# Attention and two feed-forward stages in one kernel: weight sums of the seven-product scheme taken in batch 0, one of two split anew in each batch

## The chip, the cores and the metric

One Trainium2 chip, one core. The metric is the device time of one execution in microseconds, the median of several runs.

## The reference

For 4 batches of 576 tokens with 8 heads of 64, causal attention is mixed with a memory read-out, and the result x (2304 x 512) goes through two feed-forward stages, all in float32:

```python
x = (g * mem_out + (1 - g) * local)                 # attention, 8 heads of 64 -> 512
h = (x @ w1) * (x @ w2) @ w3 @ w_out                # 512 -> 1024 -> 1024 -> 512
out = (sigmoid(x2 @ w_gate) * (x2 @ w_val)) @ w_out2  # x2 = h; 512 -> 1536 -> 512
```

## The kernel before

Float32 products are made from three fp32r matmuls: each operand is split into a high part (a cast) and a low part (the value minus the cast, `split_rows`, line 469), and high x high, low x high and high x low are summed in PSUM.

The work is four batches, one after the other (`ffn(b)`, line 506). Each has four stages that TensorE does in order: ab (x with w1 and w2, 8 tiles of 128 columns), xw (with w3 times w_out, multiplied ahead in `prep`), gv (with w_gate and w_val, 12 tiles) and ot (with the last matrix). The attention of batch b+1 is cut into small steps, which `drive` (line 943) puts between the products of ab, xw and ot of batch b; gv takes none. Batch 0 also loads all weights in their raw form, converts them (`conv_step`, line 204: VectorE, ScalarE and GpSimd in turn, into one of three buffers `wraw`), splits them (`split_step`, line 309) into a ring of slots for TensorE and stores the split form in DRAM (tiles `k`), from where the later batches fetch it (`load_step`, line 289). `pump` (line 342) takes one step of each after every product or two.

A tile of ab or gv has two weight blocks, one for each factor, and two halves of the tokens. With eight products that is 48 matmuls. The seven-product scheme (`two_rows`, line 417) needs 42, with sums of x (`token_steps`, line 395: eleven steps of subtraction and split) and, for each of 20 weight tiles, sums of the weights: four instructions (lines 270 to 273 in `make_step`), of which `lower` gives three to VectorE and one to GpSimd here. A tile then reads four slots: the plain first block, two slots with sums, and a plain block of half size. Its products come in the order 1, 6, 5, 2, 7, 3, 4: the first slot serves products 1 and 2, the second 6 and 5, the third 7 and 3, the fourth 4.

Before, batch 0 uses eight products everywhere and stores the raw weights of the 20 tiles too (`kf`, line 241). In batch 1, `make_step` fetches them (`wagain`), makes the sums, splits them into `wmade` buffers (tag r64, three of them, which parts 4 to 6 of the tokens' sums use too) and stores them (`s`, line 281), a tile's two sum slots as two transfers of 512 KB. So gv of batch 1 has seven products and ab of batch 1 has eight; batches 2 and 3 have seven in both and fetch both sum slots ready (line 302). In batches 2 and 3 the three `wraw` buffers serve as more slots, eight in all; in batch 1 there are five (`RING`).

Tile pools set who waits: a new tile in a buffer waits for the last reader of the old one. Instructions are put in order by a scheduler on all engines but TensorE, whose order from batch 0 on is the written one. All transfers are issued from SP's queue, in order.

Of the kernel before, what the change touches and what calls it, by code (L numbers as in the profile page):

```python
# [35 lines left out]
SHARE_W = (0.2, 0.5, 0.5, 0.0)  # L36
SHARE_H = (0.0, 0.0, 0.3, 0.4)
# [3 lines left out]
SHARE_S = (0.0, 0.0, 0.5, 0.0)  # L41
# [12 lines left out]
def tile_attention_memory_ffn(  # L54
# [74 lines left out]
    kept = {}  # L129
    summed = {}  # L130
    plain = {"ab": [], "xw": [], "ot": []}
    seven = {"ab": [], "gv": []}

    def unit(src, stage=None, ring=True):
        u = len(units)
        if stage:
            ks = []
            for hf in range(2):
                n = 2 * u + hf
                nb = 2 if stage == "gv" and hf == 1 else 4  # L140
# [1 line left out]
                ks.append(stored[n])
            if stage in plain:
                plain[stage] += [(t, 4, None) for t in ks]
            if stage in seven:
                kept[u] = dr.tile([128, 8, 128], F32, tag=f"kf{u}", name=f"kf{u}")
                summed[u] = [
                    dr.tile([128, 2, 4, 128], F32, tag=f"s{u}_{m}", name=f"s{u}_{m}") for m in range(2)
                ]
                a22 = ks[1] if stage == "gv" else ks[1][:, :, 2:4]  # L150
                seven[stage] += [(ks[0], 4, None), (summed[u][0], 4, u), (summed[u][1], 4, u), (a22, 2, None)]
# [24 lines left out]
    makes = [x[2] for st in ("gv", "ab") for x in seven[st][1::4]]  # L176
    second = plain["ab"] + plain["xw"] + seven["gv"] + plain["ot"]
    NSECOND = len(second)
    again = second + (seven["ab"] + plain["xw"] + seven["gv"] + plain["ot"]) * (B - 2)
# [69 lines left out]
    made = set()

    def load_kept(k):
        if k < len(makes):
            t = fp.tile([128, 8, 128], F32, tag="wraw", name=f"wagain{k}", bufs=3)
            nc.sync.dma_start(out=t, in_=kept[makes[k]])
# [2 lines left out]
    def make_step():


        k = len(made)  # L260
        if k >= len(makes):
            return False
        if ws["mstep"] == 0:
            if k == 0:
                assert not raws
                for n in range(3):
                    load_kept(n)
            a11, a12, a21, a22 = (fresh[k][:, 2 * n : 2 * n + 2] for n in range(4))
            e1, e2 = lower(SHARE_S), lower(SHARE_S)
            e1.tensor_add(a22, a21, a22)  # L270
            e2.tensor_sub(a21, a11, a21)
            e1.tensor_sub(a11, a22, a11)
            e1.tensor_sub(a12, a12, a11)
            ws["mstep"] = 1
            return True
        m = ws["mstep"] - 1
        t = fp.tile([128, 2, 4, 128], F32R, tag="r64", name=f"wmade{k}_{m}", bufs=R64)
        src = fresh[k].rearrange("p (a b) c -> p a (b c)", b=2)
        src = src[:, 0::3] if m == 0 else src[:, 1:3]
        split_rows(t.rearrange("p x (a b) c -> p x a (b c)", b=2), src, SHARE_W)  # L280
        nc.sync.dma_start(out=summed[makes[k]][m], in_=t.bitcast(F32))
        ws["mstep"] = (ws["mstep"] + 1) % 3
        if m == 1:
            made.add(makes[k])
            del fresh[k]
            load_kept(k + 3)
        return True

    def load_step():
        m = ws["again"]  # L290
        if m >= len(again):
            return False
        src, nb, u = again[m]
        late = m - NSECOND
        tag, bufs = ("wslot", RING) if late < 0 or late % (RING + 3) < RING else ("wraw", 3)
        if sum(places[x] == tag for x in slots) >= bufs:
            return False
        while u is not None and u not in made:
            make_step()
# [206 lines left out]
    def ffn(b):  # L506
        fa, fw, fo = (*FR0, 1.0) if b == 0 else (FA[b > 1], 1.0, 1.0)
        x = Xops if b > 1 else Xt

        hs = []  # L510
        for f in range(F1):
# [123 lines left out]
    def attention(b, lag):  # L635
# [238 lines left out]
        def l_part(p):  # L874
# [205 lines left out]
```

## Time and profile before

| | |
|---|---|
| median of 3 runs | 1109.21 us (1105.85 to 1110.59) |
| profiled execution, its own time | 1108.51 us |
| its span | 1106.7 us |
| TensorE (matmul) busy | 1032.6 us, 93% |
| VectorE, ScalarE, GpSimd busy | 693.2, 541.0, 521.2 us |
| moved by transfers | 281.51 MB, mean 254 GB/s |

The span runs from the first to the last instruction; the execution's own time has the launch around it. The shares are means over stages with different limits, so the stretches are read apart. PE is TensorE's matmul, PEld its weight load, DVE VectorE, ACT ScalarE, POOL GpSimd, SP the queue that issues transfers. In a row of a timeline, the bracket tells how long the engine stood idle ahead and what ended that.

### The profile page before, as it was taken

The page shows a single profiled execution, that of the slowest core. Times are in us where ns is not written, and L with a number is a line of the kernel's source. Part 1 is how long each engine was busy: PE and PEld are TensorE (multiplying, and loading weights), DVE is VectorE, ACT ScalarE, POOL GpSimd, SP SyncE. Part 2 cuts the span into 40 slices and gives each one's busy share as a digit, 9 for nine tenths or more (in the row PEclk, how much of TensorE's full clock was granted, in tenths as well). Part 3 has the DMA queues.
Part 4 walks back from the last instruction along what each step waited for, and adds up shares of the span by engine and source line. Part 5 has one row for each costly group of instructions (what it writes and reads, how often), then busy time and mean ns, then how long its engine had stood idle before and what let it go on. Part 6 is the DMA issues. An engine that isn't in the chain of part 4 may idle for free.

```text
span 1106.7 us, 20533 instructions
## 1 busy us (share of the span) xinstructions
PE 1032.6 (93%) x7304; PEld 915.1 (83%) x7304; DVE 693.2 (63%) x1566; ACT 541.0 (49%) x1174; POOL 521.2 (47%) x452
## 2 busy tenths in 40 slices
PE   6989798999999799999769999999999999999998
PEld 3555586887989789898759989987999889999998
DVE  7896898867678846877845531786466524615630
ACT  6777565645565644655533342444544432224420
POOL 5887565525656644555733322554433422324320
PEclk9999889998999899999979999999999999999999
DMA  7565579956899569989978845875389537958981
GB/s 271 164 208 197 183 262 325 328 196 240 276 320 335 202 214 390 348 330 339 347 264 315 299 146 182 281 241 176 118 298 327 196 117 253 327 202 283 329 287 56
DMA packets 103934, 281.51 MB, mean 254 GB/s; under 512 B 12568, under 2 KB 35224, under 8 KB 103832
## 3 DMA queue, kind: packets, MB, share of 16 engines
q1 hardware_dynamic: 103832, 280.20, 73.8%
q8 instruction: 58, 0.95, 0.3%
q14 instruction: 44, 0.36, 0.1%
HBM read 211.48 MB, written 68.68 MB: 253 GB/s over the span
## 4 chain that ended last, share of the span: by engine, by line
PE 65%; DVE 14%; POOL 7%; DMA 5%; issue 5%; ACT 3%; SPq 0%; DVEq 0%; POOLq 0%; ACTq 0%
PE gvp L388 16%; PE ot L377 13%; PE abp L388 8%; PE ab L377 7%; PE xw L377 5%; PE s L738 4%; PE t L799 3%; PE o L867 3%; DVE wraw L235 2%; DVE wraw L234 2%; POOL wraw L239 2%; PE wps L377 2%; POOL x L472 2%; DMA wslot<-s 2%; DVE p L743 1%
## 5 line engine op out<-in xcount | busy, mean ns | idle before, releaser
L388 PE MATMUL gvp<-x,wslot 128*128 128x288 f32 x1512 | 208.1, 298 | 22.7 <-ACT x L470 14.9
L388 PEld LDWEIGHTS gvp<-x,wslot 128*128 128x128 f32 x1512 | 204.4, 190 | 26.1 <-ACT x L470 15.1
L377 PE MATMUL ot<-hg,wslot 128*128 128x288 f32 x1152 | 166.5, 301 | 4.3 <-DVE hg L472 4.3
L377 PEld LDWEIGHTS ot<-hg,wslot 128*128 128x128 f32 x1152 | 156.2, 190 | 10.6 <-issue 5.1
L769 POOL TENSOR_SCALAR p<-p,sm,omg 116x116 f32<-116x116 f32 (+4 forms) x100 | 93.7, 940 | 144.2 <-DVE sm L767 101.8
L239 POOL TENSOR_TENSOR wraw<-wraw,cr 128x512 int32<-128x512 int32 x76 | 110.8, 1469 | 75.8 <-DVE wraw L235 40.0
L108 ACT ACTIVATE p<-p,sm 116x116 f32<-116x116 f32 (+4 forms) x160 | 93.0, 582 | 71.6 <-DVE sm L743 71.4
L377 PE MATMUL ab<-x,wslot 128*128 128x288 f32 x768 | 120.1, 307 | 0.0
L377 PE MATMUL xw<-h,wslot 128*128 128x288 f32 x768 | 115.0, 303 | 1.7 <-DVE h L472 1.3
L377 PEld LDWEIGHTS ab<-x,wslot 128*128 128x128 f32 x768 | 106.4, 192 | 7.6 <-issue 4.9
L377 PEld LDWEIGHTS xw<-h,wslot 128*128 128x128 f32 x768 | 104.9, 191 | 7.0 <-issue 3.5
L743 DVE CUSTOM_DVE_ANT_0 p<-s,msk 116x116 f32<-116x116 f32 (+4 forms) x160 | 67.7, 452 | 52.1 <-PE s L738 51.8
L388 PE MATMUL abp<-x,wslot 128*128 128x288 f32 x672 | 96.1, 299 | 0.6 <-DVE u3ab L463 0.6
L388 PEld LDWEIGHTS abp<-x,wslot 128*128 128x128 f32 x672 | 90.3, 188 | 3.6 <-issue 1.3
L799 PE MATMUL t<-idf,p 116*116 116x116 f32 x480 | 70.8, 278 | 17.2 <-DVE p L769 10.3
L377 PE MATMUL gv<-x,wslot 128*128 128x288 f32 x576 | 79.3, 297 | 5.8 <-DVE hgraw L603 4.5
L377 PEld LDWEIGHTS gv<-x,wslot 128*128 128x128 f32 x576 | 76.7, 188 | 8.3 <-DVE hgraw L603 6.5
L799 PEld LDWEIGHTS t<-idf,p 116*116 116x116 f32 x480 | 55.3, 142 | 32.2 <-issue 17.7
L440 POOL TENSOR_TENSOR u4gv<-u2gv,s5gv 128x288 f32<-128x288 f32 x36 | 30.1, 836 | 73.5 <-ACT s5gv L438 73.5
L226 ACT ACTIVATE cr<-r 128x512 int32<-128x512 uint32 x76 | 51.2, 675 | 24.5 <-POOL wraw L239 24.0
L235 DVE SCALAR_TENSOR_TENSOR wraw<-cy,wraw 128x512 int32<-128x512 int32 x76 | 60.5, 820 | 0.2
L472 POOL TENSOR_TENSOR wslot<-wraw,wslot 128x512 fp32r<-128x512 f32 x36 | 51.7, 1437 | 17.8 <-ACT wslot L470 17.1
(124 smaller groups left out, 1741.2 us busy)
## 6 DMA issues: line engine op xcount, KB each, us to landing
wslot<-k SPq DMA_DIRECT2D x128, 512.0 KB, 5.0
wslot<-s SPq DMA_DIRECT2D x104, 512.0 KB, 4.7
k<-wslot SPq DMA_DIRECT2D x48, 512.0 KB, 4.7
s<-wmade SPq DMA_DIRECT2D x40, 512.0 KB, 5.9
wslot<-k SPq DMA_DIRECT2D x52, 256.0 KB, 4.3
r<-in_gv_dram SPq DMA_DIRECT2D x24, 512.0 KB, 6.2
kf<-wraw SPq DMA_DIRECT2D x20, 512.0 KB, 5.3
wagain<-kf SPq DMA_DIRECT2D x20, 512.0 KB, 6.8
```

Source lines behind the costliest of these rows:

```text
L108: ins = nc.scalar.activation(**kw)
L226: nc.scalar.activation(out=r, in_=w[:, :, 0].bitcast(U32), func=AF.Copy, scale=2.0**-29)
L235: nc.vector.scalar_tensor_tensor(z, y, -(2**31), z, ALU.bitwise_and, ALU.bitwise_or)
L239: nc.gpsimd.tensor_tensor(z, z, tmp["r"], ALU.add)
L377: nc.tensor.matmul(ps, w[:, wi, blk, :], x[:, xi, cols : cols + n], start=first and part == 0, stop=last and part == 2,)
L388: nc.tensor.matmul(ps, w[:, wi, blk + k, :], x[:, xi, k, :], start=k == 0 and part == 0, stop=k == 1 and part == 2,)
L472: eng.tensor_sub(dst[:, 1], src, dst[:, 0].bitcast(F32))
L738: nc.tensor.matmul(os_[hh], q_[r, 0, i * T : (i + 1) * T], k_[r, 1, c0:c1], start=x == 0, stop=x == len(terms) - 1,)
L743: nc.vector.tensor_tensor_reduce(out=ps_[hh][:, c0:c1], in0=os_[hh], in1=msk[:, SP - w + c0 : SP - w + c1], scale=-0.125, scalar=3.0e38 if ...
L769: lower(SHARE_N).tensor_scalar(ps_[hh][:, :w], ps_[hh][:, :w], sm[:, 6 + hh : 7 + hh], omg[:T, 2 * p + hh : 2 * p + hh + 1], ALU.mult, ALU ...
L799: nc.tensor.transpose(tp[:T, c : c + T], src[hh][:, j * T : (j + 1) * T], idf[:T, :T])
L867: nc.tensor.matmul(ot[r, XO + q0 : XO + S], v_[:, j, hh], pt[:, hh, j].rearrange("p a c -> p (a c)")[:, q0 - X : S - X] if j < 4 else pt[: ...
```

## The change

The sums are taken in batch 0, in place in `wraw`, right after the second half of a tile was split (`take_sums`), and stored in float32 instead of the raw weights. `make_step` and the `wmade` buffers are gone. In batch 1 the stored sums are fetched into `wraw` and both sum slots are split from there straight into the ring; the first of the two (`both`) is stored split, for batches 2 and 3. The second is split anew in batches 2 and 3 too, from half a fetch (256 KB). `wraw` serves for that, so the ring has five slots in all batches. Batch 1 has seven products in ab as well, and its x gets the sums that `two_rows` reads. The second slot of ab is stored at half size. The shares that `lower` deals by and one pace of `drive` are other numbers.

```diff
-SHARE_W = (0.2, 0.5, 0.5, 0.0)
-SHARE_H = (0.0, 0.0, 0.3, 0.4)
+SHARE_W = (0.2, 0.5, 0.5, 0.5)
+SHARE_H = (0.0, 0.0, 0.4, 0.4)
-SHARE_S = (0.0, 0.0, 0.5, 0.0)
+SHARE_S = (0.0, 0.5, 0.0, 0.0)
-FA = (1.0, 0.9)
+FA = (0.9, 0.9)
...
-                nb = 2 if stage == "gv" and hf == 1 else 4
+                nb = 2 if stage in ("ab", "gv") and hf == 1 else 4
...
+            if stage in ("ab", "gv"):
+                sums[u] = dr.tile([128, 8, 128], F32, tag=f"kf{u}", name=f"kf{u}")
+                both = dr.tile([128, 2, 4, 128], F32, tag=f"s{u}", name=f"s{u}")
+                ks[1:1] = [(both, u, 0), (None, u, 1)]
+            again[stage] += ks
...
+    again = [x for st in ("ab", "xw", "gv", "ot") for x in again[st]]
+    shared = list(sums)
+    again = again + [(x[0], 4) if len(x) == 3 and x[2] == 0 else x for x in again] * (B - 2)
...
-            if hf == 1 and u in kept:
-                nc.sync.dma_start(out=kept[u], in_=raws[u])
...
+    def take_sums(u):
+        a11, a12, a21, a22 = (raws[u][:, 2 * n : 2 * n + 2] for n in range(4))
+        e1, e2 = lower(SHARE_S), lower(SHARE_S)
+        e1.tensor_add(a22, a21, a22)
+        e2.tensor_sub(a21, a11, a21)
+        e1.tensor_sub(a11, a22, a11)
+        e1.tensor_sub(a12, a12, a11)
+        nc.sync.dma_start(out=sums[u], in_=raws[u])
+
+    def load_sums(k):
+        if k < len(shared) * (B - 1):
+            t = fp.tile([128, 8, 128], F32, tag="wraw", name=f"wsums{k}", bufs=3)
+            u = shared[k % len(shared)]
+            b0, b1 = (0, 8) if k < len(shared) else (2, 6)
+            nc.sync.dma_start(out=t[:, b0:b1], in_=sums[u][:, b0:b1])
             fresh[k] = t
...
     def load_step():
         m = ws["again"]
-        if m >= len(again):
+        if m >= len(again) or len(slots) >= RING:
             return False
...
+        w = fp.tile([128, 2, 4, 128], F32R, tag="wslot", name=f"wslot{n}", bufs=RING)
+        if len(again[m]) == 2:
+            src, nb = again[m]
+            w = w[:, :, :nb]
+            nc.sync.dma_start(out=w.bitcast(F32), in_=src)
+        else:
+            to, _, which = again[m]
+            k = ws["made"]
+            src = fresh[k].rearrange("p (a b) c -> p a (b c)", b=2)
+            src = src[:, 0::3] if which == 0 else src[:, 1:3]
+            split_rows(w.rearrange("p x (a b) c -> p x a (b c)", b=2), src, SHARE_W)
+            if to is not None:
+                nc.sync.dma_start(out=to, in_=w.bitcast(F32))
+            if which == 1:
+                del fresh[k]
+                ws["made"] += 1
+                load_sums(k + 3)
...
         if hf == 1:
+            if u in sums:
+                take_sums(u)
             del raws[u]
...
-        x = Xops if b > 1 else Xt
+        x = Xops if b > 0 else Xt
...
-            if b > 1:
+            if b > 0:
                 yield from two_rows(take(4), x, f"ab{b}_{f}", ht, hraw, False, 6.0 * fa)
...
-            while b == 1 and d == KC - 1 and make_step():
-                pass
...
-            if b == 1:
-                pending.append(lambda: tail(b, p, xp, SHARE_X))
-            elif p % 2 == 1:
+            if p % 2 == 1:
                 groups = token_steps(f"x{b}", *state["xf"], Xnext)
```

**Order, first place: VectorE in gv of batch 0**, one tile's time. `cy` and `wraw` belong to the conversion of a weight, `wslot` to its split, `hgraw` and `hg` to the products. Before:

```order
L603 TENSOR_TENSOR hgraw_3_3597<-gv_3_1_1_3660,gsb_3_1_3658 128x288
L472 TENSOR_TENSOR wslot_3698<-wraw_3515,wslot_3698 128x512
L234 TENSOR_SCALAR wraw_3695<-cy_3677 128x512
L234 TENSOR_SCALAR wraw_3695<-cy_3718 128x512
L472 TENSOR_TENSOR hg_3_3596<-hgraw_3_3597,hg_3_3596 128x576
L235 SCALAR_TENSOR_TENSOR wraw_3695<-cy_3677,wraw_3695 128x512
L235 SCALAR_TENSOR_TENSOR wraw_3695<-cy_3718,wraw_3695 128x512
L603 TENSOR_TENSOR hgraw_4_3687<-gv_4_0_1_3711,gsb_4_0_3709 128x288
L225 TENSOR_SCALAR cy_3808<-r_67_3681 128x512
L603 TENSOR_TENSOR hgraw_4_3687<-gv_4_1_1_3750,gsb_4_1_3748 128x288
L472 TENSOR_TENSOR wslot_3788<-wraw_3605,wslot_3788 128x512
```

Now:

```order
L227 TENSOR_SCALAR wraw_3917<-cy_3940 128x512
L581 TENSOR_TENSOR hgraw_7_4003<-gv_7_1_1_4065,gsb_7_1_4063 128x288
L228 SCALAR_TENSOR_TENSOR wraw_3917<-cy_3899,wraw_3917 128x512
L228 SCALAR_TENSOR_TENSOR wraw_3917<-cy_3940,wraw_3917 128x512
L244 TENSOR_TENSOR wraw_3823<-wraw_3823 128x256
L218 TENSOR_SCALAR cy_3993<-r_70_3850 128x512
L452 TENSOR_TENSOR hg_7_4002<-hgraw_7_4003,hg_7_4002 128x576
L581 TENSOR_TENSOR hgraw_8_4097<-gv_8_0_1_4121,gsb_8_0_4119 128x288
L452 TENSOR_TENSOR wslot_4108<-wraw_3917,wslot_4108 128x512
L246 TENSOR_TENSOR wraw_3823<-wraw_3823 128x256
L247 TENSOR_TENSOR wraw_3823<-wraw_3823 128x256
L581 TENSOR_TENSOR hgraw_8_4097<-gv_8_1_1_4159,gsb_8_1_4157 128x288
```

Three instructions on `wraw` of 128x256 have come in for each tile, on the buffer of the tile before the one that is converted.

**Second place: ScalarE at the start of gv in batch 1.** `x_1_0` to `x_1_6` are the seven parts of the tokens that the products need, `s1gv` and `s5gv` copies of products out of PSUM. Before:

```order
L470 CAST wmade_1_5991<-wagain_5828 128x512
L438 COPY s5gv_0_6646<-gvp_0_5_6639 128x288
L470 CAST wmade_0_6042<-wagain_5878 128x512
L470 CAST wmade_1_6067<-wagain_5878 128x512
L470 CAST wmade_0_6097<-wagain_5943 128x512
L470 CAST wmade_1_6127<-wagain_5943 128x512
L470 CAST x_1_4_6579<-x2f_1_6216 128x576
L470 CAST x_1_5_6612<-x2f_1_6216 128x576
L470 CAST x_1_6_6616<-x2f_1_6216 128x576
L108 ACT_TABLE_LOAD
```

Now:

```order
L450 CAST x_1_5_6495<-x2f_1_6001 128x576
L410 COPY s1gv_0_6511<-gvp_0_1_6504 128x288
L418 COPY s5gv_0_6529<-gvp_0_5_6522 128x288
L450 CAST wslot_6550<-wsums_5729 128x512
L450 CAST wslot_6563<-wsums_5729 128x512
L450 CAST x_1_6_6499<-x2f_1_6001 128x576
L108 ACT_TABLE_LOAD
```

The five casts into `wmade` ahead of x_1_4 to x_1_6 are gone; two casts into ring slots stand ahead of x_1_6.

**Third place: SP in gv of batch 3.** `s` is a sum slot that is fetched ready, `k` a plain slot, `kf` the stored sums. Before:

```order
L302 DMA wslot_12222<-s_0_156 128x1024
L302 DMA wslot_12211<-k_153 128x1024
L302 DMA wslot_12234<-s_1_157 128x1024
L302 DMA wslot_12250<-k_154 128x2x256
L302 DMA wslot_12291<-k_158 128x1024
L302 DMA wslot_12302<-s_0_161 128x1024
L302 DMA wslot_12314<-s_1_162 128x1024
L302 DMA wslot_12330<-k_159 128x2x256
L302 DMA wslot_12382<-s_0_166 128x1024
```

Now:

```order
L271 DMA wslot_9925<-k_142 128x2x256
L271 DMA wslot_9941<-k_145 128x1024
L271 DMA wslot_9982<-s_148 128x1024
L271 DMA wslot_10008<-k_146 128x2x256
L255 DMA wsums_9996<-kf_159 128x512
L271 DMA wslot_10024<-k_149 128x1024
L271 DMA wslot_10065<-s_152 128x1024
L255 DMA wsums_10079<-kf_163 128x512
L271 DMA wslot_10091<-k_150 128x2x256
```

Where two ready sum slots of 512 KB were fetched for a tile there is one now, and a fetch of 256 KB of unsplit sums into `wsums` for a tile three further on.

## Rows read from the trace of the kernel before

**Rows 1.** Table by stretch (us; busy time and count by engine, clock, DMA share, GB/s).

```profile
140.00:250.00 110.00, 103.68 (x714) 88.20 (x714) 86.29 (x188) 64.63 (x139) 54.95 (x45) 0.97 0.81 278
291.60:372.60 81.00, 75.77 (x552) 73.51 (x553) 63.93 (x102) 46.52 (x89) 49.98 (x34) 1.00 0.91 315
428.85:690.86 262.01, 240.06 (x1798) 218.62 (x1797) 163.15 (x376) 123.78 (x273) 117.07 (x103) 0.97 0.82 293
690.86:924.42 233.56, 230.18 (x1751) 210.02 (x1749) 131.97 (x346) 105.67 (x238) 97.06 (x89) 1.00 0.65 218
924.42:1103.20 178.78, 176.55 (x1322) 175.62 (x1320) 73.32 (x157) 51.94 (x108) 52.23 (x54) 1.00 0.75 256
```

**Rows 2.** Timeline of TensorE, gv of batch 1 (start, length, what, idle before).

```profile
545.10 1.23 PE L388 MATMUL gvp<-x,wslot 128*128 128x288 f32 x8
...
563.17 0.85 PE L388 MATMUL gvp<-x,wslot 128*128 128x288 f32 x2 [14.89 <-ACT x L470]
...
576.76 5.83 PE L388 MATMUL gvp<-x,wslot 128*128 128x288 f32 x42 [0.49 <-DMA wslot<-s]
...
595.29 11.43 PE L388 MATMUL gvp<-x,wslot 128*128 128x288 f32 x84 [0.99 <-DMA wslot<-s]
...
636.35 0.56 PE L377 MATMUL ot<-hg,wslot 128*128 128x288 f32 x3
```

**Rows 3.** Timeline of TensorE, gv of batch 2.

```profile
796.88 2.84 PE L388 MATMUL gvp<-x,wslot 128*128 128x288 f32 x20
...
804.18 62.40 PE L388 MATMUL gvp<-x,wslot 128*128 128x288 f32 x466 [0.92 <-POOL x L472]
866.42 0.56 PE L377 MATMUL ot<-hg,wslot 128*128 128x288 f32 x3
```

**Rows 4.** Timeline of ScalarE, start of gv in batch 1.

```profile
557.92 0.62 ACT L470 CAST wmade<-wagain 128x512 fp32r<-128x512 f32 x1 [1.95 <-DMA s<-wmade]
559.11 0.67 ACT L470 CAST x<-x2f 128x576 fp32r<-128x576 f32 x1 [0.57 <-DMA s<-wmade]
562.45 0.67 ACT L470 CAST x<-x2f 128x576 fp32r<-128x576 f32 x1 [2.66 <-DMA s<-wmade]
```

**Rows 5.** Costliest groups: GpSimd's part of a weight split (busy us, mean ns).

```profile
L472 POOL TENSOR_TENSOR wslot<-wraw,wslot 128x512 fp32r<-128x512 f32 x36 | 51.7, 1437 | 17.8 <-ACT wslot L470 17.1
```

**Rows 6.** Groups by line and shape: the sums, lines 270 to 273.

```profile
L271 POOL TENSOR_TENSOR wagain<-wagain 128x256 f32<-128x256 f32 x20 | 15.9, 794 | 28.4 <-DVE wagain L270 14.5 <-issue 10.6 <-DVE sm L767 1.5
...
L272 DVE TENSOR_TENSOR wagain<-wagain 128x256 f32<-128x256 f32 x20 | 14.3, 714 | 9.7 <-POOL wagain L271 9.7
...
L273 DVE TENSOR_TENSOR wagain<-wagain 128x256 f32<-128x256 f32 x20 | 13.0, 650 | 0.4
...
L270 DVE TENSOR_TENSOR wagain<-wagain 128x256 f32<-128x256 f32 x20 | 11.0, 551 | 8.9 <-DMA wagain<-kf 8.9
```

**Rows 7.** Timeline of TensorE, two tiles of gv in batch 0.

```profile
323.27 6.63 PE L377 MATMUL gv<-x,wslot 128*128 128x288 f32 x48 [0.49 <-DVE hgraw L603]
330.29 6.62 PE L377 MATMUL gv<-x,wslot 128*128 128x288 f32 x48 [0.40 <-DVE hgraw L603]
```

**Rows 8.** Timeline of VectorE, the same tiles of batch 0.

```profile
327.24 0.76 DVE L234 TENSOR_SCALAR wraw<-cy 128x512 int32<-128x512 int32 x2 [1.19 <-POOL wslot L472]
```

**Rows 9.** Instructions on tile wagain: ns shortest/median/longest, first and last start.

```profile
L272 DVE TENSOR_TENSOR wagain<-wagain x20: 408/426/1648, 405.0 to 553.8; 128x256 f32<-128x256 f32 x20
```

**Rows 10.** Chain of waits in gv of batch 1 (start, us, what).

```profile
572.30 4.32 DMA wslot<-s
...
578.62 4.11 DMA wslot<-s
...
590.33 4.82 DMA wslot<-s
```

**Rows 11.** Landing of tile wslot's transfers: 566 to 634 us, then 760 to 790.

```profile
DMA to landing us min/median/max: 3.1/4.3/5.6
...
DMA to landing us min/median/max: 3.0/3.2/3.6
```

More of the change, by code (lines that the diff above doesn't have):

```diff
@@ L128, in tile_attention_memory_ffn @@
     stored = {}
[L129 to L132, printed above, removed]
+    sums = {}
+    again = {"ab": [], "xw": [], "gv": [], "ot": []}
     def unit(src, stage=None, ring=True):
@@ L139, in unit @@
                 n = 2 * u + hf
-                nb = 2 if stage == "gv" and hf == 1 else 4
+                nb = 2 if stage in ("ab", "gv") and hf == 1 else 4
                 stored[n] = dr.tile([128, 2, nb, 128], F32, tag=f"k{n}", name=f"k{n}")
[L142 to L151, printed above, removed]
+                ks.append((stored[n], nb))
+            if stage in ("ab", "gv"):
[3 more added lines that the diff above has]
+            again[stage] += ks
         units.append((src, ring))
@@ L175, in tile_attention_memory_ffn @@
         unit(halves(o2[:, u]), "ot")
[L176 to L179, printed above, removed]
+    again = [x for st in ("ab", "xw", "gv", "ot") for x in again[st]]
+    shared = list(sums)
+    again = again + [(x[0], 4) if len(x) == 3 and x[2] == 0 else x for x in again] * (B - 2)
     NU = len(units)
@@ L186, in tile_attention_memory_ffn @@
     wot = {}
-    ws = {"conv": 0, "step": 0, "split": 0, "ring": 0, "freed": 0, "use": 0, "again": 0, "mstep": 0, "wo": 0, "pass": 0, "wready": False}
+    ws = {"conv": 0, "step": 0, "split": 0, "ring": 0, "freed": 0, "use": 0, "again": 0, "made": 0, "wo": 0, "pass": 0, "wready": False}
     tmp = {}
@@ L244, in conv_step @@
         return True
-    places = {}
     fresh = {}
[L249 to L254, printed above, removed]
-            fresh[k] = t
[L257 to L287, printed above, removed]
@@ L289, in load_step @@
     def load_step():
         m = ws["again"]
-        if m >= len(again):
+        if m >= len(again) or len(slots) >= RING:
             return False
[L293 to L299, printed above, removed]
-        n = ws["ring"]
-        w = fp.tile([128, 2, 4, 128], F32R, tag=tag, name=f"wslot{n}", bufs=bufs)[:, :, :nb]
@@ L302, in load_step @@
-        nc.sync.dma_start(out=w.bitcast(F32), in_=src)
+        if m == 0:
+            assert not raws
+            for k in range(3):
+                load_sums(k)
+        n = ws["ring"]
+        w = fp.tile([128, 2, 4, 128], F32R, tag="wslot", name=f"wslot{n}", bufs=RING)
[15 more added lines that the diff above has]
+                load_sums(k + 3)
@@ L303, in load_step @@
         slots[n] = w
-        places[n] = tag
         ws["ring"] += 1
@@ L334, in split_step @@
             slots[n] = w
-            places[n] = "wslot"
             ws["ring"] += 1
         if hf == 1:
+            if u in sums:
+                take_sums(u)
             del raws[u]
@@ L344, in pump @@
         split_step()
-        if phase["n"] == 2:
-            make_step()
     def need(store, s):
@@ L618, in ffn @@
                         pump()
-                        if pending:
+                        if pending and ws["conv"] >= NU:
                             pending.pop(0)()
@@ L1010, in tile_attention_memory_ffn @@
         phase["n"] = min(b + 1, 3)
-        ftot = 384 * FR0[0] + 144 * FR0[1] + 288 + 42.4 * (8 - NPREP) if b == 0 else (384, 336, 336)[b - 1] * FA[b > 1] + 432.0
+        ftot = 384 * FR0[0] + 144 * FR0[1] + 288 + 42.4 * (8 - NPREP) if b == 0 else 336 * FA[b > 1] + 432.0
         drive(ffn(b), chain(atts[b + 1], atts[b + 2]) if b + 1 < B else None, ftot, ATOT, FRAC)
```

## The prediction

> **What bounds the kernel now.** I first read the table of busy time by stretch [rows 1]. It cuts the part behind the start into two stretches of batch 0 and into batches 1, 2 and 3. In batches 2 and 3 TensorE is busy 230.2 of 233.6 us and 176.6 of 178.8 us: only fewer products could shorten them, and any new wait lengthens them. Batch 1 takes 262.0 us, 28.4 us more than batch 2, for the same work but for eight products in place of seven in its ab stage. Batch 0 is different: in its gv stage VectorE is busy 63.9 of 81.0 us, in its ab stage 86.3 of 110.0 us, the fullest of the engines beside TensorE.
>
> The timeline of TensorE says where batch 1 loses time. Its gv stage runs from 545.10 to 636.35, 91.25 us [rows 2]; that of batch 2 from 796.88 to 866.42, 69.54 us for the same 504 matmuls [rows 3]. One gap alone is 14.89 us, and ScalarE's cast of x ends it. ScalarE's timeline shows why [rows 4]: the casts of x wait for the stores of made sums (DMA s<-wmade), because both lie in the three buffers of tag r64. The rest of gv in batch 1 has gaps of 0.49 and 0.99 us that end with the fetch of a sum slot (wslot<-s) [rows 2]; batch 2, which had three more slots, has none in 62.40 us [rows 3].
>
> From 62.40 us for 466 matmuls [rows 3] I take 0.134 us for a matmul of 288 columns: seven products (42 matmuls) take 5.62 us, eight take 6.43 us.
>
> **Batch 1.** (a) The ab stage goes from 384 to 336 matmuls: 48 x 0.134 = **6.4 us less**, on TensorE's path. Its extra vector work is that of ab in batch 2, where TensorE hides it [rows 1]. (b) The sums are no longer made, stored and fetched in batch 1. The order of ScalarE shows x_1_4 and x_1_5 with no such cast ahead of them, and two casts ahead of x_1_6. With the makes gone, gv should come down to batch 2's 69.54 us: **21.7 us less**. (c) Not all of that stays. The cast of x_1_6 now stands behind a cast into a slot that TensorE frees only after its product 2: a cast (0.62 us [rows 4]), the cast of x and its subtraction come to some 2 us, with two products (1.6 us) and an old gap of 0.9 us [rows 3] against them; I take 1.3 us. And both sum slots of all 20 weight tiles are now split in front of their use: two casts of 0.62 us, one subtraction on VectorE and one on GpSimd (1437 ns, the same shape in batch 0 [rows 5]) in the 5.62 us of a tile. ScalarE and GpSimd have this time in batch 2's row (busy 106 and 97 of 234 us [rows 1]). What it costs is a product's evacuation that stands behind it; between 0 and one cast (0.62 us) for each tile I take 0.125 us, 2.5 us in all, near the lower end since three accumulators rotate and a product takes 0.8 us. **3.8 us more**. Batch 1 together: 24.3 us less.
>
> **Batch 0.** Sums for 20 tiles, 12 of gv and 8 of ab, move here. The same four instructions stood in batch 1 and have rows [rows 6]: on VectorE 551, 714 and 650 ns, 1.92 us a tile; on GpSimd 794 ns. In gv a tile now takes 7.02 us (from 323.27 to 330.29) where TensorE needs 6.43 [rows 7]. VectorE and GpSimd wait for each other in it: VectorE stands 1.19 us until GpSimd has ended a weight's subtraction, and only then rewrites a buffer [rows 8], to which GpSimd then adds. The change reorders this loop: a tile's buffer is now free only when its sums are stored, and the three sums of one tile stand on VectorE between the rewriting of two others. With 12 x 1.92 = 23 us added to 63.9 busy of 81.0, VectorE has at least 5.9 us too little in gv if every duration stays; the 8 tiles in ab (15.4 us) fit into its 23.7 idle us but stand in order in front of the products' evacuations. From below the cost is 0: with each sum at its shortest, near 0.41 us [rows 9], 12 x 1.23 = 15 us fit into the 17 idle ones. From above it is all 20 x 1.92 = 38 us. I take 8 us for gv (0.67 a tile, so a period near 7.7) and 4 us for ab, a quarter of its added work: **12 us more**, nearer the lower end because VectorE idles 1.5 us in each tile's period now. The GpSimd sum fits: GpSimd is busy 50 of 81 us. Token sums of batch 1's x (eleven steps in place of four splits) run in the last 22 us of batch 0's ot stage, where batch 2's are hidden already: 0. Stores of sums replace stores of raw weights one for one, and ab's second slot is stored at half size: 0 or a little gain.
>
> **Batches 2 and 3.** Now five slots serve where eight did. What is late then is the first sum slot. It goes into the buffer that product 2 frees, and product 6 of the next tile wants it. Batch 1 before had five slots, and its chain shows the pace [rows 10]: the fetch at 572.30 takes 4.32 us and work goes on at 576.76; the next is issued at 578.62, 1.86 us later. A tile needs 5.62 us, so a fetch of up to 3.76 us is hidden, and each us beyond is paid. In that stretch landings are 3.1/4.3/5.6 us (shortest, median, longest), with two fetches issued together; alone, in batch 2's xw stage, 3.0/3.2/3.6 [rows 11]. Now one 512 KB fetch stands there by itself, since the second sum slot is split from a buffer that was loaded three tiles ahead. I take 3.9 us, a little above the middle of the two medians: 0.14 us a tile. Tiles without attention between: 8 of ab in batch 3 and 24 of gv: 32 x 0.14 = **4.5 us more**. Bounds: 0 (3.2 us) and 32 x 1.06 = 34 us (4.82, the longest in the chain [rows 10]). The 40 new splits (half of them GpSimd's) lie beside products with 5.6 us for each. [...]
>
> **The sum.** Against the profiled execution's 1108.5 us (span 1106.7; the median of three is 1109.2): -6.4 - 21.7 + 3.8 + 12 + 4.5 = -7.8 us, so **1101 us**. 0.5% (5.5 us) is about what a measurement of this kernel can tell from no change.
>
> **The rivals.**
> 1. *Batch 0 gives everything back (slower).* Place: VectorE in ab and gv of batch 0. A sum there takes 0.41 us or up to 1.65 us [rows 9], the long ones under a GpSimd instruction; GpSimd is busy 62% of gv. If the sums are paid in full, +38 instead of +12: 1127 us. It decides from 20 us on, where the gain is gone. For it: 23 us of work against 17 idle; against it: VectorE's present waits are for GpSimd, and part of the sums falls into them. The Trainium skill (SBUF — State Buffer, Who interferes with whom) speaks for it: a VectorE instruction with two inputs in SBUF is blocked, not slowed, while GpSimd reads there. The trace agrees with 1.65 against 0.41 us. Chance 0.18.
> 2. *The ring of five is too short.* Fetches of 4.6 us, as paired ones had, cost 0.84 us in each of 32 tiles, 27 us instead of 4.5: 1123 us. For it: the gaps in batch 1; against it: less traffic at that moment. Chance 0.12.
> 3. *Batch 0 hides its sums.* VectorE's idle time takes them (+3), batches 2 and 3 lose 1 us: 1088 us. Chance 0.20.
> 4. *The change does not do what it says in batch 1*: splits in front of use hold x at the start of gv as the makes did, and 14 us of the gain stay away: 1115 us. The new order of ScalarE speaks against it. Chance 0.07.
> The forecast itself, 1094 to 1109, has 0.43.
>
> **How the numbers follow.** Faster by over 0.5% (below 1103.7): 0.30 of the forecast's 0.43 and all of rival 3, 0.50. Within: 0.13 of the forecast and 0.09 from the edges of rivals 1, 2 and 4, 0.22. Slower: the rest of rivals 1, 2 and 4, 0.28. For 8 in 10 the range leaves out the far halves of rivals 1 and 2 and the edge of 3: 1086 to 1124.
>
> **What would show it.** Right: batch 1 near 238 us with seven products in ab and no gap above 3 us at the start of gv; batch 0's gv at 7.5 to 8 us a tile; gaps of some 0.1 to 0.3 us that end with the fetch of a sum slot in gv of batches 2 and 3. Wrong: a period of 8.5 us or more in batch 0 with VectorE above 95% (rival 1), gaps of 0.8 us in every tile of batches 2 and 3 (rival 2), or the ab stage of batch 0 as long as before with gv at 7.0 us a tile (rival 3).

## The result and the profile after

The change makes the kernel slower by 1.1%: 1121.02 us (1118.84 to 1123.63, four runs) against 1108.97 (1105.85 to 1110.59, four), ratio 1.0113 [1.008, 1.0146]. Forecast: 1101. The profiled execution took 1122.1 us, its span 1120.3, 13.6 us longer than before.

Lengths of stages, here and in the experiments below, come from one profiled execution of each kernel. Where the code of a batch is the same they still differ: batches 2 and 3 took 433.1 us in the change, 430.8 in e3 and 433.2 in e6; batch 1 took 262.0 us before and 259.4 in e4. Differences of 2 to 3 us in a batch therefore say nothing by themselves.

Stage lengths from TensorE's timeline, from a stage's first product to the next stage's (before → after, us):

| | ab | xw | gv | ot | batch | forecast |
|---|---|---|---|---|---|---|
| batch 0 | 117.0 → 116.2 | 42.1 → 41.0 | 85.0 → 97.0 | 56.2 → 58.1 | +12.1 | +12 |
| batch 1 | 82.3 → 67.8 | 33.9 → 41.6 | 91.2 → 76.2 | 54.5 → 57.2 | −19.2 | −24.3 |
| batch 2 | 64.5 → 66.5 | 41.5 → 41.6 | 69.5 → 76.6 | 58.0 → 57.0 | +8.2 | } +4.5 |
| batch 3 | 44.8 → 50.1 | 26.1 → 26.8 | 69.5 → 76.1 | 38.3 → 38.3 | +12.5 | |

In batch 1, ab and xw have to be read together: attention steps moved from ab into xw (61 of their matmuls stand in xw before, 121 after).

The table of busy time by stretch, after (columns as in [rows 1]; first gv of batch 0, then batches 1, 2, 3):

```profile
291.60:372.60 81.00, 70.31 (x485) 67.50 (x484) 79.66 (x113) 38.65 (x74) 48.34 (x38) 0.96 0.77 265
441.04:683.84 242.80, 234.53 (x1751) 210.79 (x1749) 154.97 (x369) 124.79 (x279) 127.93 (x108) 1.00 0.65 220
683.84:925.63 241.79, 233.59 (x1750) 210.54 (x1749) 139.64 (x357) 116.30 (x258) 108.56 (x98) 1.00 0.59 188
925.63:1116.90 191.27, 181.79 (x1322) 177.53 (x1320) 79.84 (x167) 62.55 (x127) 64.36 (x63) 0.99 0.67 216
```

Against [rows 1], VectorE in gv of batch 0 went from 63.9 to 79.7 of 81.0 us: it is full, and TensorE does 485 matmuls where it did 552. TensorE stood idle 3.4 of 233.6 us in batch 2 and now 8.2 of 241.8, in batch 3 2.2 and now 9.5. That is 12.1 us of the 20.7 that these batches lost. The rest counts as busy time of the same matmuls: behind a gap the profile gives 42 of them 5.83 us, where a row without gaps gives them 5.62, and a part of gv in batch 3 ran at the lower clock (0.98 in that stage).

**Batch 0.** TensorE's timeline, gv of batch 0, after; these two tiles take 8.51 us each, from 312.01 to 320.52 and to 329.03, where one took 7.02 [rows 7]:

```profile
312.01 6.63 PE L357 MATMUL gv<-x,wslot 128*128 128x288 f32 x48 [1.34 <-DVE hgraw L581]
320.52 8.13 PE L357 MATMUL gv<-x,wslot 128*128 128x288 f32 x48 [1.88 <-DVE hgraw L581]
329.03 6.62 PE L357 MATMUL gv<-x,wslot 128*128 128x288 f32 x48 [0.37 <-DVE hgraw L581]
```

The middle tile spends 8.13 us on its 48 matmuls because TensorE ran part of it at the lower of its two clock levels, 1.2 GHz (granted clock 0.50 from 322.0 to 325.4), behind the gap of 1.88 us. That is not what lengthens the stage: in e5 the clock stays at 1.00 from 291.6 to 372.6, and gv of batch 0 takes 97.0 us too.

Groups by line and shape, after: the three of the four sums that VectorE does (count | busy us, mean ns | idle before).

```profile
L247 DVE TENSOR_TENSOR wraw<-wraw 128x256 f32<-128x256 f32 x20 | 14.2, 710 | 0.2
L246 DVE TENSOR_TENSOR wraw<-wraw 128x256 f32<-128x256 f32 x20 | 12.6, 629 | 2.7 <-POOL wraw L245 2.5
L244 DVE TENSOR_TENSOR wraw<-wraw 128x256 f32<-128x256 f32 x20 | 10.1, 507 | 2.6 <-POOL wslot L452 2.6
```

They take 1.85 us a tile on VectorE, as a mean of all 20 tiles; from [rows 6] 1.92 was expected. The size was right. Over the twelve tiles gv grew by 12.0 us, 1.0 us a tile: a little over half of these 1.85.

**Batch 1.** TensorE's timeline, start of gv, after (up to 565 us, where the last row is cut off):

```profile
550.41 2.94 PE L368 MATMUL gvp<-x,wslot 128*128 128x288 f32 x20
554.08 3.04 PE L368 MATMUL gvp<-x,wslot 128*128 128x288 f32 x18 [0.72 <-DVE x L452]
558.70 6.53 PE L368 MATMUL gvp<-x,wslot 128*128 128x288 f32 x47 [1.59 <-DVE x L452]
```

The gap of 14.89 us [rows 2] is gone; two gaps of 0.72 and 1.59 stand there. A slow stretch in and behind the old gap went with it: before, the granted clock was 0.50 (1.2 GHz) from 552.2 to 569.2, and the 21 matmuls from 563.17 on took 5.39 us. Later in that stage two rows of VectorE's timeline show a cost the forecast had at 0.125 us a tile:

```profile
606.66 1.87 DVE L452 TENSOR_TENSOR hg<-hgraw,hg 128x576 fp32r<-128x576 f32 x1
608.46 0.45 DVE L436 TENSOR_TENSOR u4gv<-gvp,u4gv 128x288 f32<-128x288 f32 x1
```

and one of GpSimd's, over the same time:

```profile
606.63 1.28 POOL L452 TENSOR_TENSOR wslot<-wsums,wslot 128x512 fp32r<-128x512 f32 x1
```

Here a new split's subtraction on GpSimd lies over VectorE's subtraction for hg, which takes 1.87 us; where GpSimd idles beside it 0.75 (gv of batch 2, VectorE's timeline):

```profile
833.78 0.75 DVE L452 TENSOR_TENSOR hg<-hgraw,hg 128x576 fp32r<-128x576 f32 x1
```

The product's evacuation u4 stands behind it, and TensorE's timeline in gv of batch 1 names u4:

```profile
608.96 5.89 PE L368 MATMUL gvp<-x,wslot 128*128 128x288 f32 x42 [0.37 <-DVE u4gv L436]
```

**Batches 2 and 3.** TensorE's timeline, gv of batch 2, after. In place of 62.40 us in one piece [rows 3] nearly every tile of 42 matmuls (5.83 us) has a gap:

```profile
820.04 5.83 PE L368 MATMUL gvp<-x,wslot 128*128 128x288 f32 x42 [0.37 <-DVE u3gv L443]
826.17 5.83 PE L368 MATMUL gvp<-x,wslot 128*128 128x288 f32 x42 [0.31 <-DMA wslot<-s]
832.25 5.83 PE L368 MATMUL gvp<-x,wslot 128*128 128x288 f32 x42 [0.26 <-DMA wslot<-s]
838.57 5.83 PE L368 MATMUL gvp<-x,wslot 128*128 128x288 f32 x42 [0.49 <-DVE hgraw L444]
```

The chain of waits there (start, us, what) alternates between two causes:

```profile
826.17 1.84 PE gvp L368 x12
828.03 4.09 DMA wslot<-s
...
832.25 2.65 PE gvp L368 x18
834.92 0.63 ACT wslot L450
835.55 0.07 issue
835.62 0.61 POOL wslot L452
836.23 0.64 issue
836.87 0.81 POOL s5gv L437
837.69 0.02 issue
837.71 0.45 DVE u3gv L443
838.16 0.38 DVE hgraw L444
```

First cause: 12 matmuls (products 6 and 5), then the fetch of the next first sum slot, then, 6.08 us after 826.17, product 6 of the next tile. Second: 18 matmuls (up to product 2), then the split of the second slot; s5 waits behind its subtraction on GpSimd, and u3 and hgraw, which free an accumulator, behind s5. The landings of wslot in this stretch (805 to 865 us), after:

```profile
DMA to landing us min/median/max: 3.4/4.3/5.7
```

The fetch of the sum slot is not alone in flight. SP's timeline has three other transfers within 4 us behind it, and the stage moves 245 GB/s:

```profile
828.03 0.32 SPq L271 DMA_DIRECT2D wslot<-s  x1
830.24 0.32 SPq L255 DMA_DIRECT2D wsums<-kf  x1
830.62 1.17 SPq L271 DMA_DIRECT2D wslot<-k  x2
```

TensorE's waits in batches 2 and 3, after (us in total, times, longest):

```profile
PE gvp L368 <- DMA wslot<-s: 2.9, 8, 0.6
...
PE gvp L368 <- DVE hgraw L444: 1.8, 4, 0.5
PE abp L368 <- DVE hraw L444: 1.8, 4, 0.5
...
PE abp L368 <- DMA wslot<-s: 1.0, 2, 0.6
```

With three single waits on L443 and L445 (0.4, 0.8 and 0.6 us), fetches of sum slots end ten gaps (3.9 us) and evacuations eleven (5.4 us). At the start of the two gv stages the waits for parts of x come to 5.5 us, where they were 3.6.

### The profile page after: what moved, and what is told of

It is laid out like the page before. It is cut to its first block, busy times and chain, and to the rows that moved or that the text cites. A ratio compares the mean times of both kernels' runs of the same rounds, so it can differ in the third digit from the quotient of the medians.

```text
span 1120.3 us, 20565 instructions
## 1 busy us (share of the span) xinstructions
PE 1045.5 (93%) x7256; PEld 915.7 (82%) x7256; DVE 747.8 (67%) x1629; ACT 562.2 (50%) x1217; POOL 578.1 (52%) x492
## 4 chain that ended last, share of the span: by engine, by line
PE 57%; DVE 21%; DMA 7%; issue 6%; ACT 4%; POOL 4%; SPq 0%; DVEq 0%; POOLq 0%; ACTq 0%
PE ot L357 13%; PE gvp L368 12%; PE xw L357 8%; PE abp L368 5%; PE ab L357 4%; PE s L716 4%; DMA wslot<-s 4%; PE t L777 3%; DVE wraw L228 3%; PE o L845 3%; DVE wraw L227 2%; PE wps L357 2%; DVE wslot L452 2%; DVE p L721 2%; DMA wslot<-k 2%
## 5 line engine op out<-in xcount | busy, mean ns | idle before, releaser
L368 PE MATMUL gvp<-x,wslot 128*128 128x288 f32 x1512 | 212.3, 299 | 16.9 <-DVE x L452 4.9
L357 PE MATMUL ot<-hg,wslot 128*128 128x288 f32 x1152 | 169.2, 302 | 6.0 <-DVE hg L452 3.8
L368 PE MATMUL abp<-x,wslot 128*128 128x288 f32 x1008 | 150.0, 300 | 5.2 <-DVE hraw L444 1.8
L368 PEld LDWEIGHTS abp<-x,wslot 128*128 128x128 f32 x1008 | 136.1, 188 | 13.6 <-DVE u3ab L443 3.3
L357 PE MATMUL xw<-h,wslot 128*128 128x288 f32 x768 | 116.2, 303 | 2.1 <-DMA wslot<-k 1.1
L357 PE MATMUL gv<-x,wslot 128*128 128x288 f32 x576 | 83.0, 304 | 11.8 <-DVE hgraw L581 11.3
L357 PEld LDWEIGHTS gv<-x,wslot 128*128 128x128 f32 x576 | 79.9, 195 | 14.8 <-DVE hgraw L581 14.2
L450 ACT CAST wslot<-wsums 128x512 fp32r<-128x512 f32 x80 | 48.9, 621 | 31.6 <-PE gvp L368 13.5
L228 DVE SCALAR_TENSOR_TENSOR wraw<-cy,wraw 128x512 int32<-128x512 int32 x76 | 63.8, 861 | 0.3
L357 PE MATMUL ab<-x,wslot 128*128 128x288 f32 x384 | 60.2, 309 | 1.3 <-DVE hraw L517 1.3
L452 POOL TENSOR_TENSOR wslot<-wsums,wslot 128x512 fp32r<-128x512 f32 x40 | 54.0, 1349 | 12.2 <-ACT wslot L450 11.9
```

The source lines that it names most:

```text
L228: nc.vector.scalar_tensor_tensor(z, y, -(2**31), z, ALU.bitwise_and, ALU.bitwise_or)
L357: nc.tensor.matmul(ps, w[:, wi, blk, :], x[:, xi, cols : cols + n], start=first and part == 0, stop=last and part == 2,)
L368: nc.tensor.matmul(ps, w[:, wi, blk + k, :], x[:, xi, k, :], start=k == 0 and part == 0, stop=k == 1 and part == 2,)
L450: nc.scalar.copy(dst[:, 0], src)
L452: eng.tensor_sub(dst[:, 1], src, dst[:, 0].bitcast(F32))
```

## The experiments

**e1, both slots fetched ready, five slots kept.** Batch 1 stores the second sum slot split as well; batches 2 and 3 split nothing.

```diff
-                both = dr.tile([128, 2, 4, 128], ...)
-                ks[1:1] = [(both, u, 0), (None, u, 1)]
+                both = [dr.tile([128, 2, 4, 128], ...) for m in range(2)]
+                ks[1:1] = [(both[0], u, 0), (both[1], u, 1)]
...
-    again = again + [(x[0], 4) if len(x) == 3 and x[2] == 0 else x for x in again] * (B - 2)
+    again = again + [(x[0], 4) if len(x) == 3 else x for x in again] * (B - 2)
...
-        if k < len(shared) * (B - 1):
+        if k < len(shared):
```

> The changed kernel, but batch 1 stores both sum slots split, and batches 2 and 3 fetch both ready: no split is left in batches 2 and 3, the ring keeps its five slots. The changed kernel lost 20.7 us in batches 2 and 3 (gv 76.6 and 76.1 us where it was 69.5 and 69.5, ab of batch 3 50.1 where it was 44.8). Theory F (the fetch of the first sum slot comes too late with five slots): gv stays at 75 to 78 us in both, the total at 1119 to 1125 us. Theory S (the new splits hold up the evacuation of products): gv goes back to 70 us, the total to 1100 to 1104 us.

Measured: 1131.57 us, ratio 1.0188 [1.0138, 1.0237]. Batches 2 and 3 took 426.0 us, against 433.1 in the change and 412.3 before: without the 40 splits they are 7.1 us shorter. Their gv took 72.9 and 74.3 us, between the two theories. But gv of batch 1 grew from 76.2 to 83.0 with the second store. The profiled execution took 1124.52 us, 7 us less than the median; where the other executions lost that time no trace shows.

**e2, e1 with eight slots in batches 2 and 3**, as before the change.

```diff
+        late = m - NSECOND
+        tag, bufs = ("wslot", RING) if late < 0 or late % (RING + 3) < RING else ("wraw", 3)
...
```

> As the run with both sum slots ready, and in batches 2 and 3 the three raw buffers serve as slots again, eight in all. Both theories: gv at 69.5 to 70.5 us in batches 2 and 3, the total at 1098 to 1103 us, under the kernel before, as batch 0 costs 12 us and batch 1 gives 19. If it stays above 1108 us, neither the ring nor the splits are the cause, and the change has hurt batches 2 and 3 in another way (the pace of the attention steps).

Measured: 1122.43 us, 1.0116 [1.0085, 1.0147]. Batches 2 and 3 took 414.1 us, gv 70.0 and 69.6: three slots more are worth 11.9 us, with both sum slots of a tile fetched, and 1.8 of the 20.7 are left. The total missed its forecast, since gv of batch 1 rose to 89.7 (83.0 in e1, whose code for batch 1 is the same; the difference is not explained). The chain of waits in gv of batch 1, e2, shows plain slots late:

```profile
565.58 6.60 DMA wslot<-k
580.24 7.24 DMA wslot<-k
596.22 7.81 DMA wslot<-k
```

Waits of SP's queue in gv of batch 1 (us in total, times, longest), the change:

```profile
SPq L280 <- DVE wslot L452: 36.3, 10, 5.2
```

and e2:

```profile
SPq L287 <- DVE wslot L460: 44.0, 11, 7.1
```

A store of a split slot waits at SP for the subtraction, and the fetches stand behind it in order. Either this queue or the second slot's bytes could make the fetches late; e7 asks which.

**e3, the sums' arithmetic left out**, everything else kept.

```diff
-        e1.tensor_add(a22, a21, a22)
-        e2.tensor_sub(a21, a11, a21)
-        e1.tensor_sub(a11, a22, a11)
-        e1.tensor_sub(a12, a12, a11)
```

> The changed kernel without the four instructions that take the sums in batch 0; the raw weights are stored in their place and split as if they were sums, so the products of batches 1 to 3 are others. Theory V (VectorE's time for the sums makes batch 0 longer): gv of batch 0 goes from 97 back to 85 to 87 us, the total to 1109 to 1112 us. Theory W (the raw buffer that is held until the store behind the split has landed makes it longer): gv of batch 0 stays at 93 to 97 us, the total at 1117 to 1121 us.

Measured: 1107.31 us, 0.998 [0.9962, 0.9998]. In gv of batch 0 (table by stretch, e3):

```profile
291.60:372.60 81.00, 75.68 (x551) 73.20 (x551) 62.28 (x100) 46.35 (x89) 49.76 (x35) 1.00 0.91 313
```

VectorE is back at 62.3 us, TensorE at 551 matmuls, the stage at 85.3. It is the sums' arithmetic that costs batch 0 its 12 us, and not the stores by themselves. The edit takes out GpSimd's sum too, and the stores' wait for the sums. So it does not tell VectorE's time from the longer time for which a tile's buffer is held.

**e4, the kernel before with five slots everywhere.**

```diff
-        tag, bufs = ("wslot", RING) if late < 0 or late % (RING + 3) < RING else ("wraw", 3)
+        tag, bufs = "wslot", RING
```

> The kernel before with five slots in batches 2 and 3 too, both sum slots fetched ready as it does: one edit. Theory F: gv of batches 2 and 3 at 75 to 78 us in place of 69.5, ab of batch 3 at 48 to 51 in place of 44.8, the total at 1125 to 1132 us. Theory S: no more than 1 to 3 us longer than the kernel before, 1109 to 1112 us.

Measured: 1123.02 us, 1.0108 [1.0066, 1.0151]. Batches 2 and 3 took 428.9 us, 16.5 more than before, with nothing else changed. That is over twice the 7.1 us that batches 0 and 1 together gain by the change, though here two sum slots are fetched for a tile, and in the change one.

**e5, the roles of the sum slots exchanged**: the first is split anew, the second stored.

```diff
-                ks[1:1] = [(both, u, 0), (None, u, 1)]
+                ks[1:1] = [(None, u, 0), (both, u, 1)]
...
```

> The changed kernel with the two sum slots exchanged in batches 2 and 3: the first one (products 6 and 5) is split anew from the raw buffer that was loaded three tiles ahead, the second one (products 7 and 3) is fetched ready. Ring of five, one split and one fetch of 512 KB a tile as before. Theory F (the fetch into the slot that frees last is late): that slot no longer waits for a fetch, so gv of batches 2 and 3 comes to 71 to 74 us in place of 76.6 and 76.1, ab of batch 3 to 46 to 48 in place of 50.1, the total to 1111 to 1116 us. Theory S (a split ahead of the evacuations is what costs): nothing is gained, 76 to 77 us, as in batch 1 where both are split (76.2), the total at 1119 to 1124 us.

Measured: 1122.97 us, 1.012 [1.009, 1.015]. Batches 2 and 3 gained 8.8 us (gv 74.2 and 72.7), batch 1 lost 10 (gv 86.5). In gv of batch 2 it is the plain first slot that is late now (chain of waits, e5):

```profile
816.15 5.76 DMA wslot<-k
827.92 5.78 DMA wslot<-k
```

So with five slots, in both roles, some fetch is short of lead; which one sets the price. Batch 1 lost its 10 us with one store a tile, as in the change, and at 233 GB/s in gv, where the change moves 276. Waits of SP's queue in that stage, e5:

```profile
SPq L273 <- DMA s<-wslot: 43.9, 10, 5.7
```

Fetches wait there for the store of a split slot to land. More bytes are not needed to make this stage long.

**e6, ScalarE takes all of the conversion's `cy` steps in batch 0.**

```diff
-SHARE_Y = (1.0, 0.4, 0.0, 0.0)
+SHARE_Y = (1.0, 1.0, 0.0, 0.0)
```

> The changed kernel with the first step of the conversion (cy) always on ScalarE in batch 0, where VectorE had six in ten of them. VectorE is busy 98% of gv in batch 0 with the sums, ScalarE 49%. Theory V: it takes 1.2 us a tile off VectorE, so gv of batch 0 goes from 97 to 88 to 92 us, the total to 1112 to 1117 us. Theory W (the held buffer and its store set the pace): gv stays at 95 us or more, the total at 1118 to 1122 us.

Measured: 1113.54 us, 1.0039 [1.0019, 1.0058], the total expected from relieving VectorE. The place was not: gv came down by 1.7 us only (97.0 to 95.3, and not at all in e8 and e10), VectorE still at 76.5 of 81.0:

```profile
291.60:372.60 81.00, 69.73 (x490) 66.72 (x490) 76.53 (x108) 46.68 (x89) 52.44 (x39) 0.98 0.84 280
```

Ten `cy` of 1.22 us are gone from VectorE in this stretch, but its subtraction for hg went from 1.02 to 1.30 us in the mean and the sum of L246 from 0.62 to 1.08. So VectorE's load alone does not set the length of gv. The rest came in ab, xw and ot of batch 0 (3.8, 2.9 and 4.5 us), less 4 us of a later start.

**e7, e2 with the stores issued later**, four calls of `pump` after the split.

```diff
-            if to is not None:
-                nc.sync.dma_start(out=to, in_=w.bitcast(F32))
+            if to is not None:
+                owing.append([4, to, w])
...
```

> The run with both sum slots ready and eight slots, with one edit: the stores of the split slots in batch 1 are issued four products later. In that run gv of batch 1 took 89.7 us in place of 76.2, with gaps that end with fetches of plain slots; SP stood 44 us in that stage waiting for a subtraction in front of a store, the fetches behind it. Theory Q (the queue: a store that waits for its split holds up the fetches behind it): gv of batch 1 at 74 to 78 us, the total at 1098 to 1104 us by the profiled execution. Theory B (the bytes: a store more in each tile is more than the transfers can carry): gv of batch 1 stays at 84 to 90 us, the total at 1108 to 1114.

Measured: 1118.64 us, 1.0105 [1.0071, 1.014]; gv of batch 1 91.1. SP waited as long as in e2 for subtractions:

```profile
SPq L338 <- DVE wslot L466: 45.0, 11, 6.6
```

The edit did not take away the wait that it was to test. Queue or bytes stays open for e2; e5 shows that this stage can get as long without more bytes.

**e8, e7 with e6.**

> The late stores and cy on ScalarE together. If theories V and Q both hold: batch 0 is 5 to 9 us shorter than in the changed kernel and gv of batch 1 no longer than there, the total at 1092 to 1098 us, faster than the kernel before by 1 to 1.5%. If only V holds 1103 to 1108, if neither 1112 or more.

Measured: 1111.07 us, 1.0002 [0.9981, 1.0024]. e6's edit gives the same on top of e7 (−7.6 us), and gv of batch 1 at 90.8 still eats the ring's gain.

**e9, product 2 right behind product 1** in `two_rows`, for all tiles of a stage but its first (whose x is not all ready then), with the plain slot released there and the first sum slot after product 5.

```diff
         p1 = product(1, 0, 0, 0)
...
+        p2 = product(2, 0, 2, 5)
+        release(s)
...
         p6 = product(6, 1, 0, 2)
...
         p5 = product(5, 1, 2, 1)
+        release(s + 1)
...
-        p2 = product(2, 0, 2, 5)
-        release(s)
-        release(s + 1)
```

> The changed kernel with product 2 done second in place of fourth, in every tile but the first of a stage: 1, 2, 6, 5, 7, 3, 4. The first slot is then free two products (1.6 us) sooner, and the slot that goes into its buffer has 5.6 us less its weight load in place of 3.8. Nothing else is moved. Theory F (the first sum slot's fetch has too little time with five slots): no gap in batches 2 and 3 ends with such a fetch, gv there at 70 to 73 us in place of 76.6 and 76.1, ab of batch 3 at 45 to 47 in place of 50.1, the total at 1105 to 1111 us. Theory S (the splits hold up evacuations): gv of batches 2 and 3 at 75 us or more, the total at 1118 to 1123 us.

Measured: 1112.78 us, 1.0029 [1.0015, 1.0042]; batches 2 and 3 425.5 us, 7.6 less than in the change. The gv stages took 75.6 and 72.1 us, ab of batch 3 48.1, so the expected 70 to 73 and 45 to 47 came only in part. ScalarE's timeline in gv of batch 2, e9, has the copies behind products 1 and 5:

```profile
825.14 0.40 ACT L410 COPY s1gv<-gvp 128x288 f32<-128x288 f32 x1 [0.65 <-PE gvp L368]
...
827.54 0.40 ACT L433 COPY s5gv<-gvp 128x288 f32<-128x288 f32 x1
```

and SP's has the fetch between them:

```profile
825.88 0.32 SPq L271 DMA_DIRECT2D wslot<-s  x1
```

In the change that fetch went out at 828.03, behind product 5. Now product 2 frees a slot before product 6 starts, the fetch has the whole tile of 5.6 us, and TensorE has rows of a hundred matmuls again:

```profile
798.46 20.90 PE L368 MATMUL gvp<-x,wslot 128*128 128x288 f32 x142 [0.58 <-DVE x L463]
...
820.02 15.47 PE L368 MATMUL gvp<-x,wslot 128*128 128x288 f32 x114 [0.66 <-DVE c11gv L416]
```

No gap in these gv stages ends with hgraw any more either, though a tile's split still starts behind its fourth product; why is not shown.

**e10, e9 with e6.**

> Product 2 second and, in batch 0, cy on ScalarE, which alone made the changed kernel 7.5 us faster. If both are independent: 1098 to 1104 us, faster than the kernel before by 0.5 to 1%. If the order of products gains nothing, 1113 us as with cy alone.

Measured: 1105.15 us (1099.78 to 1107.24, seven runs), 0.9946 [0.9926, 0.9966]: 0.5% under the kernel before, where the change is 1.1% above it; just outside the 1098 to 1104 expected. Batch 3, e10:

```profile
911.72:1094.59 182.87, 178.02 (x1322) 175.81 (x1320) 79.82 (x167) 61.52 (x127) 65.95 (x63) 1.00 0.68 226
```

TensorE stands idle 4.9 us in it, where it was 9.5 in the change and 2.2 before. The profiled execution (1099.78 us) is the fastest of the seven.

**e11, e4 with e9's order.**

> The kernel before with five slots in batches 2 and 3 (1123 us, gv 76.8 and 74.8 us) and product 2 second. No split stands in these batches, so it shows the fetch alone. Theory F: gv of batches 2 and 3 back at 69.5 to 71 us, that of batch 1 from 88.4 to 82 to 85 (its gap for the makes stays), the total at 1104 to 1111 us. If the bytes in flight and not the time of the fetch set the pace, gv stays at 74 us or more, the total at 1118 or more.

Measured: 1111.12 us, 1.0012 [0.9994, 1.003]; batches 2 and 3 421.3 us, 7.5 less than e4. The order gives the same 7.5 us without the change's splits and sums, so it is the ring's lead that it mends. It mends less than half of e4's 16.5 us: gv took 71.3 and 74.1 us, ab of batch 3 48.4. The fetches of sum slots got longer with the lead, 5.1 us in the median of gv of batch 2 where e4 has 4.6, and those that still end a gap there took 5.7 to 5.8. The expected gain in gv of batch 1 did not come (91.3). The profiled execution (1118.4 us) is the slowest of ten, 7 us above the median.

**e12, the kernel before with e9's order.**

> The kernel before with product 2 second and nothing else, eight slots in batches 2 and 3. Theory F: batches 2 and 3 stay as they are (69.5 us of gv), gv of batch 1, which has five slots, loses its small gaps, 4 to 7 us, the total at 1102 to 1106 us. It is the yardstick for what the change itself is worth once the order of products is better.

Measured: 1106.02 us, 0.9956 [0.9936, 0.9975]. The expected 4 to 7 us in gv of batch 1 did not come (91.4 us). The profiled execution, 1109.47 us, is the slowest of the six and no shorter than the one before, so it cannot show where the others gained. The 0.4% is measured and not explained. It is nearly as large as e10's gain over the kernel before (0.54%), so that e10 beats e12 is not shown.

## Why the prediction was wrong

The step that failed is "batches 2 and 3: 4.5 us more": they lost 20.7 us. The step has two parts, both mis-sized.

- *The fetch.* The mechanism was right (12 matmuls, then a fetch, then the wait), and e4 shows that five slots alone lengthen these batches. It was priced as 3.9 us against 3.76 hidden; in gv of batch 2 the fetches that TensorE waited for took 4.05 to 4.32. By the forecast's own formula 4.15 gives 0.39 x 32 = 12.5 us; e1 against e2 measured 11.9. I had held that the paired fetches of [rows 10] (4.1 to 4.8) were slow because paired, and that the fetch now "stands there by itself". No second sum slot is fetched with it, but three other transfers are in flight, and the stage moves 245 GB/s; the 3.2 us of [rows 11] came from a stretch (760 to 790 us) that moves 74. Rival 2 had the mechanism right and this size at twice. One detail was wrong: the buffer is freed by product 5, not by product 2, as the issue at 828.03 shows; the 1.86 us came from a row and were right. With all of it on five slots the kernel before pays 16.5 (e4).
- *The 40 splits*, "beside products with 5.6 us for each", taken at 0: 7.1 us (the change against e1). Busy shares gave them room; the order on each engine put s5, u3 and hgraw behind them, and eleven gaps of TensorE end with such an evacuation.

11.9 + 7.1 + 1.8 left over = 20.7 us (to rounding) in place of 4.5: 16 of the 21 us by which the profiled execution (1122.1) missed; batch 1 is the other 5. The parts hold for this order of taking them away: in e1 and e2 a tile fetches both sum slots, in the change one. In the change itself the two causes stand in each other's place, with ten gaps (3.9 us) and eleven (5.4 us), so how the loss divides between them there is not shown.

Batch 0: forecast +12, measured 12.1, but the split into gv +8 and ab +4 was wrong: gv paid all 12.0, ab gave 0.8 back. That the sum came out is luck. Rival 1's sign (VectorE above 95%) came true, and in some tiles its period of 8.5 us, but not its price of 38: a third of the 20 x 1.85 = 37 us is paid, nothing of it in ab. The rule of the Trainium skill that was cited for it (SBUF — State Buffer, Who interferes with whom) agrees with the durations (1.87 us under a GpSimd instruction against 0.75 without), but did not make the sums cost their whole time.

Batch 1: forecast −24.3, measured −19.2. The fewer products and the end of the 14.89 us gap are there. gv stopped at 76.2 instead of 73.3: the splits cost more than 0.125 us a tile, as the 1.87 us subtraction shows. ab, xw and ot together gave 4.2 us where 6.4 were counted.

The Trainium skill (DMA: Bandwidth & Descriptors, Anatomy of one DMA) gives 2.0 us plus the bytes over 436 GB/s for a transfer that GpSimd issues; for 512 KB that would be an estimate of 3.2 us. These fetches are issued by SP, so it does not price them: they took 4.05 to 4.32 us where the stage moves 245 GB/s, and plain ones 6.6 to 7.8 in gv of batch 1 in e2, at 299 GB/s.

Not settled: whether the second slot's store slows batch 1 in e1 and e2 by SP's queue or by its bytes (e7 failed to part them; e5 shows that bytes are not needed); what in the sums' arithmetic lengthens gv of batch 0, VectorE's time or the held buffer; the price of the splits with eight slots; why e6's gain lies outside gv; the 9.0 us that e11 leaves of e4's loss; e12.

## What to carry to other kernels

A ring's depth is lead time: compare the time from the read that frees a slot to the read that wants it again with the landing measured in *that* stage, among the transfers that will be in flight, and remember that moving the freeing read earlier buys lead for no memory (e9, e11: 7.5 us), though the fetches of e11 grew longer with it. An engine that is busy half the time can still delay: work that lies "beside" the products must be followed on its queue, up to the evacuation that stands behind it. The busy share does not give the price of added work: sums moved into gv of batch 0, with VectorE 79% busy, were paid at half of their duration (12.0 us for 12 x 1.85), and in ab, with VectorE 78% busy (86.3 of 110.0 us), at nothing.

## What the runs showed of the hardware

A VectorE subtraction of 128x576 took 0.75 us alone and 1.87 us when it began 0.03 us behind a GpSimd subtraction of 1.28 us: 1.12 us more, nearly the other's whole length. A fetch of 512 KB had no single duration. It took 3.2 us in batch 2's quiet xw stage before, at 74 GB/s [rows 11], and 4.2 us (median of the sum slots) in gv of batch 2 of the change, at 245 GB/s. In the same stage before, at 311 GB/s, it took 5.2 us, and eight slots hid it. TensorE's clock fell to its lower level, 1.2 GHz, in the gap of 14.89 us before and for parts of gv of batch 0 after; there the 16 matmuls from 322.0 to 325.4 took 3.40 us, where 16 take 2.1 at the upper level (5.62 us for 42).
